# Three modulation vectors moved from the sets of steps 8 and 16 into those of steps 16, 32, 40 and 48

## The chip, the cores and the metric

The kernel runs on one core of one Trainium2 chip. The metric is the time of one execution on the device in microseconds (us); the median of several runs counts. The core has a matmul engine (TensorE, PE in the profile, PEld for its loads of weights), VectorE (DVE), ScalarE (ACT), GpSimd (POOL) and SyncE (SP), which issues nearly all DMAs here. The engines run side by side, each with its own queue in order, and wait for each other by semaphores.

## The reference

```python
def _A_ref(u, ...):                       # S4D: a long convolution along the 2048 tokens
    dt = exp(log_dt); A = -exp(log_A_real) + 1j * A_imag; C = (C_real + 1j * C_imag) * dt[:, None]
    P = exp((A * dt[:, None])[:, :, None] * pos)
    K = 2.0 * einsum("dn,dnl->dl", C, P).real            # 448 channels, 256 states, 2048 taps
    y = irfft(rfft(u_t, 4096) * rfft(K, 4096))[:, :, :2048]
    return y + u * D_skip
def _B_ref(x, w1, b1, w2, b2):            # mixer MLP along the tokens, 2048 -> 1792 -> 2048
    return (gelu(layernorm(x)^T w1 + b1) w2 + b2)^T

mod = (silu(c) @ w_mod).reshape(1, 6, 1, 448)
sa, ca, ga, sb, cb, gb = mod[:, 0], ..., mod[:, 5]
x = A_u                                                  # (1, 2048, 448)
x = x + ga * _A_ref(layernorm(x) * (1 + ca) + sa, ...)
x = x + gb * _B_ref(layernorm(x) * (1 + cb) + sb, ...)
```

The six vectors of 448 elements that `c` and `w_mod` (448 x 2688) give are the subject here: `mod[0]` to `mod[5]` are sa, ca, ga, sb, cb, gb. The first three are needed in the convolution, the last three (sb, cb, gb) in the MLP at the end.

## The kernel before

The first half of the kernel makes the taps K of the convolution for 28 groups of 16 channels, in 56 steps (`s` from 0 to 55, two for each group). Every eight steps (`BATCH`) form a set. At the start of a set stands a window: for each of its eight steps TensorE makes exponents (`st_exponents`, L687, through `halves`, L667), ScalarE takes their exponential (`st_exp`, L696, two of 128x512 for each step, tile `mag`), GpSimd makes `st_mag2` (L712, L717). The windows of steps 0, 8, 16, 24 and 32 are `window(s)`, those of 40 and 48 `late_window(s)`; `e` counts the eight passes. After it each step turns phases (`st_phase`, L667 again) into sines (`st_step`: ScalarE L729 to L735) and these into the tiles `E` (VectorE, L739 to L743) and `G` (GpSimd, L737, L738). `E` and `G` have three rooms each in the pool `gp_`. `st_kgen` (L764) multiplies them into PSUM two steps later (one step later from step 33 on), and `st_s1` (L802, L808) begins the Fourier transform of the taps.

Between these runs everything else, put by hand into the order of TensorE, ScalarE, VectorE and GpSimd:

- `chain(q)`, small VectorE work on the parameters of the next groups (`more(n)` takes its next n pieces; L415 to L489, split on GpSimd at L404 and L406, written to DRAM at L410). In the window its pieces stand between the passes.
- `u_rows` (L591 on TensorE, L595 on VectorE, written at L597 as `yu_d<-yt`, three tiles `yt`) in the steps from 8 to 16: the input's transform, which reads `mod[1]*mod[2]` and the tile `xt` of the input; then `u_cols` (L627, L631) from step 17, which reads `mod[0]*mod[2]` and what `u_load` (L617, tile `yi`) fetches.
- `pc_load` (L828, L841), `pc_s2` (L872), `pc_mul` (L880), `pc_inv` (L895) and `pc_out` (L905, L902) from step 33: the product of the two spectra and its inverse. `piece(...)` does one of these; in the late windows it stands in passes 3 and 5.
- `warm(n)` (L679) and `idle(n)` (L685): n matmuls on constants whose results nobody reads.

`act` and `dve` are lists of work that is put off to the next `flush`, which for the windows comes once in each pass. The PSUM pool `pms` (tag `ms`) has three rooms that the modulations, `u_rows`, `u_cols`, `st_s1` and the pieces share.

A modulation has two halves, `modulation(k, 0)` and `modulation(k, 1)`. The first multiplies a broadcast copy of silu(c) (`scb`) with the weights of vector k (four matmuls of 112 rows into four quarters of a PSUM tile `pm`, L537), and a copy takes it to the tile `parts` (L539). The second adds the four quarters by a matmul with `sums` (L533), and a copy takes it, with 1 added for k of 1 and 4, to `mod[k]` (L534). The weights are 784 KB for each k, loaded by `wm_load` (L341), for k of 0 to 2 into a tile that is reused for spectra later (`wm0`), for k of 3 to 5 into rows of `xt` that `u_rows` has read:

```python
if s == 8 and e in (3, 4):
    modulation(0, e - 3)
if s == 8 and e == 5:
    G.tensor_tensor(mod[0], mod[0], mod[2], ALU.mult)
for k, e0 in ((4, 1), (5, 3), (3, 6)) if s == 16 else ():
    if e in (e0, e0 + 1):
        modulation(k, e - e0)
```

Vectors 1 and 2 are made in steps 4 to 7. SyncE's order is written out by hand up to step 8; from there to the second half a planner orders its DMAs by when its own model of the kernel has them ready.

After the 56 steps come the rest of the spectral products, the layer norm with `mod[3]` and `mod[4]` (L1455, L1456) and the MLP (L1400 to L1402, L1563 to L1565), which take the second half of the time.

Of the kernel before, what the change touches and what calls it, by code (L numbers as in the profile page):

```python
# [11 lines left out]
F32 = mybir.dt.float32  # L12
F32R = mybir.dt.float32r
BF16 = mybir.dt.bfloat16
AF = mybir.ActivationFunctionType
# [7 lines left out]
P = 128  # L23
# [209 lines left out]
def tile_adaln_s4d_mixer(ctx, tc, i, out):  # L233
# [19 lines left out]
    with ExitStack() as es:  # L253
# [85 lines left out]
        def wm_load(k, tile):  # L339
            wms[k] = tile  # L340
            nc.sync.dma_start(wms[k], i["w_mod"][:, k * D : (k + 1) * D].rearrange("(q p) d -> p q d", p=PP))  # L341
# [11 lines left out]
        def wm_slot(k):  # L353
            w = wm0.rearrange("p k d -> p (k d)")[0:PP]
            return w[:, 4 * D * (k % 4) : 4 * D * (k % 4 + 1)].rearrange("p (q d) -> p q d", q=4)
# [3 lines left out]
        late = {  # L359
            4: lambda: wm_load(2, wm_slot(2)),  # L360
            7: lambda: [
                wm_load(0, wm_slot(0)),
                nc.sync.dma_start(svt, i["SV"]),
                s2_load(0),
                s2_load(1),
# [2 lines left out]
                nc.sync.dma_start(wu, i["WU"]),  # L368
                nc.sync.dma_start(wc, i["WC"].rearrange("p (c m) -> p c m", c=2)),
            ],  # L370
            12: lambda: wm_load(4, xt[0:PP, 0:4, 0:D]),
            13: lambda: wm_load(5, xt[0:PP, 4:8, 0:D]),
            14: lambda: wm_load(3, xt[0:PP, 8:12, 0:D]),
        }


        dt = qp.tile([P, 4], F32, name="dt")
# [140 lines left out]


        sc = qp.tile([PP, 4], F32, name="sc")  # L520
        scb = qp.tile([PP, 4, 32], F32, name="scb")
        sums = qp.tile([P, P], F32, name="sums")
        G.memset(sums, 0.0)
        for q in range(4):
            G.memset(sums[32 * q : 32 * q + 1], 1.0)
# [3 lines left out]
        def modulation(k, half):  # L529

            pm = pms.tile([P, D], F32, tag="ms", name="pm")
            if half:
                T.matmul(pm, sums, pmods.pop(k), start=True, stop=True)  # L533
                act.append(lambda: S.activation(mod[k], pm, AF.Copy, bias=1.0 if k in (1, 4) else 0.0))  # L534
                return
            for q in range(4):
                T.matmul(pm[32 * q : 32 * q + 32], scb[:, q], wms[k][:, q], start=True, stop=True)  # L537
            pmods[k] = qp.tile([P, D], F32, tag="parts", name="parts")
            act.append(lambda: S.copy(pmods[k], pm))  # L539


        mv = xp.tile([P, 16, 2], F32, name="mv")
# [131 lines left out]
        def warm(n):  # L674

            g = made_k[0] // 2
            free = (kgs[g - 1] if g - 1 in kgs else kg_tile(g))[:, 4:8]
            for _ in range(n):
                T.matmul(free, ones[:, 0:P], ones[:, 0:256], start=made_k[0] % 2 == 0, stop=made_k[0] % 2 == 0, skip_group_check=True)  # L679
# [392 lines left out]
        def late_window(s):  # L1072

            flush(hold)
            for e in range(BATCH):
                st_exp(s + e)
                if e + 1 < BATCH:
                    st_exponents(s + e + 1)
                else:
                    st_phase(s)  # L1080
                mellow()
                flush(dve)
                flush(act)
                if e == 1:
                    st_kgen(s - 1, dve)
                elif e in (3, 5):
                    piece(False, True)
                st_mag2(s + e)
            st_s1(dve)
            flush(dve)  # L1090

        def window(s):
            if s:
                aside.append(True)
            angle()
            logs(s == 8)
            if s == 8:
                more(10)
                u_scale()
                u_table(0)  # L1100
                u_table(1)

            if s == 0:
                st_exponents(s)
            for e in range(BATCH):
                st_exp(s + e)

                if e + 1 < BATCH:
                    st_exponents(s + e + 1)
                else:  # L1110
                    st_phase(s)
                mellow()
                flush(dve)
                flush(act)
                if s == 8 and e == 0:
                    tt(mod[1], mod[1], mod[2], ALU.mult)
                if s < 32:
                    more(WPACE[s // 8][e])
                if s == 0 and e >= 4:
                    u_stats(e - 4)  # L1120
                if s == 8 and e in (3, 4):
                    modulation(0, e - 3)
                if s == 8 and e == 5:

                    G.tensor_tensor(mod[0], mod[0], mod[2], ALU.mult)
                if s and e < (2 if s <= 32 else 1):
                    st_kgen(s - (2 if s <= 32 else 1) + e)
                elif e == 5 and s < 24:
                    if s == 8:
                        yks[0] = y0.tile([P, 32, DC], F32, tag="yk", name="yk0")  # L1130
                    st_s1(act)

                for k, e0 in ((4, 1), (5, 3), (3, 6)) if s == 16 else ():
                    if e in (e0, e0 + 1):
                        modulation(k, e - e0)

                if s == 8 and e == 0:
                    warm(7)
                if s == 8 and e == 1:
                    u_means()  # L1140
                if s in (8, 16):
                    some(u_rows, rows, ((0, 2, 2, 2, 2, 0, 2, 2) if s == 8 else (2, 2, 2, 2, 2, 0, 1, 1))[e])
                elif s == 24 and e in (0, 2, 4, 6, 7):
                    some(u_cols, cols, 1)

                if s == 0 and e > 1:
                    st_mag2(e - 2)
                elif s and (e < 2 or s >= 32):
                    st_mag2(s + e)
                if s == 0 and e == 3:  # L1150
                    for r in range(4):
                        dsk_copy(r)
            aside.clear()
            if s == 8:
                flush(dve)
            if s >= 24 and st_s1(dve):
                flush(dve)
            if s == 0:

                S.activation(one, one, AF.Sin)  # L1160
# [5 lines left out]
        for s in range(NHALF):  # L1166
# [33 lines left out]
            if True:  # L1200
                if s < 32 and s % BATCH > 1:
                    st_kgen(s - 2)
                if s % BATCH == 1 or s < 24 and s % BATCH == 0:
                    warm(10)
                if (s + 1) % BATCH:
                    st_phase(s + 1)
                elif s + 1 < NHALF:
                    st_exponents(s + 1)
                if s == 7:
                    warm(10)  # L1210

                due.extend(soon)
                soon.clear()
                if s > 32 and s % BATCH:
                    st_kgen(s - 1, soon)
                if s in (40, 48):
                    piece(True)
                    flush(dve)
                st_step(s, between)
                if s in (40, 48):  # L1220
                    piece(False, True)
# [3 lines left out]

            if s in (1, 2):
                x_load(4 + 4 * s, 4, G)
            if s in (23, 31):
                idle(10)
            held = s > 32 and s % BATCH == BATCH - 2  # L1230
# [366 lines left out]
```

## Time and profile before

| what | value |
|---|---|
| runs | 663.93, 664.15, 666.26 us; median 664.15 |
| profiled execution | 663.85 us, span 662.1 us |
| mean clock granted to TensorE | 0.984 |
| busy, of the span | PE 612.3 us (92%), PEld 442.9, DVE 443.0 (67%), ACT 439.9 (66%), POOL 269.5 (41%) |
| weights of modulations | 6 loads of 784 KB, issued by SyncE between 32.9 and 106.1 us |
| matmuls of modulations | L537 x48 and L533 x12, from 43.4 to 131.2 us |

The span is the time from the first to the last instruction. Times in rows are in us from the start of the span. A row of the timeline has start, length, engine, line, operation, tile written and tiles read, shape and count, and in brackets how long the engine stood idle before it and what ended that. A row of the chain has start, length and the piece of work: it is the sequence of work that ended last, followed back from the end, so only what stands on it makes the kernel longer. A row of busy times has a stretch, its length, for each engine the busy us and the number of instructions, the share of the clock that TensorE got, and the mean share of the DMA engines with their GB/s (a share over 1 comes from counting a transfer where it starts). The letter q behind an engine means its queue.

### The profile page before, as it was taken

The numbers are of one execution on the slowest core, as the hardware profiler recorded it, in microseconds if no ns is written. First come the engines' busy times: TensorE is split into PE (matmuls) and PEld (weight loads), VectorE is DVE, ScalarE is ACT, GpSimd is POOL, SyncE is SP. The second block draws the span as 40 slices with busy tenths as digits, with TensorE's granted clock in tenths as the row PEclk, the third lists the DMA queues.
The fourth block names the chain that finished last, engine by engine and source line by source line (L and its number), as shares of the span: only waits on it lengthen the run. The fifth ranks groups of instructions, "written<-read, shape, count | busy, mean of one in ns | idle before, by whom it ended". The sixth has DMA issues, their size and how long they took to land.

```text
span 662.1 us, 19161 instructions
## 1 busy us (share of the span) xinstructions
PE 612.3 (92%) x7639; PEld 442.9 (67%) x7639; DVE 443.0 (67%) x853; ACT 439.9 (66%) x828; POOL 269.5 (41%) x351
## 2 busy tenths in 40 slices
PE   1878998999999999999888999999999999999997
PEld 0444555445455565656544577788999999999996
DVE  8989889689894887868655688777422553333331
ACT  5978888899989999999587678885222522222220
POOL 7785597588599788787563000000000000000000
PEclk9998999989999999999999899999999999999999
DMA  6595747598775557576787999946755275555530
GB/s 145 156 219 166 253 143 257 182 248 268 218 247 178 103 166 218 169 215 182 234 274 227 257 247 234 233 112 196 201 160 153 57 209 164 162 160 166 161 106 28
DMA packets 97858, 123.67 MB, mean 187 GB/s; under 512 B 13717, under 2 KB 79801, under 8 KB 97769
## 3 DMA queue, kind: packets, MB, share of 16 engines
q1 hardware_dynamic: 97032, 120.02, 64.2%
q0 software_dynamic: 736, 2.43, 1.5%
q8 instruction: 60, 0.98, 0.7%
q14 instruction: 30, 0.24, 0.1%
HBM read 88.33 MB, written 33.59 MB: 184 GB/s over the span
## 4 chain that ended last, share of the span: by engine, by line
PE 63%; DMA 11%; DVE 9%; ACT 7%; POOL 4%; issue 4%; SPq 3%; ACTq 0%; DVEq 0%; POOLq 0%
PE o L1563 7%; PE o L1565 7%; PE o L1564 7%; PE acc L1400 6%; PE acc L1401 6%; PE acc L1402 6%; PE xe L667 6%; PE kg L764 6%; DMA w<-in_B_w_dram 3%; PE xg L667 3%; DMA xt<-in_A_u_dram 3%; DMA v_d<-vt 3%; PE pu L591 2%; PE vv L895 2%; PE kx L872 2%
## 5 line engine op out<-in xcount | busy, mean ns | idle before, releaser
L218 ACT CAST whi<-w 128x896 fp32r<-128x896 f32 x64 | 59.7, 939 | 138.5 <-PE o L1564 82.7
L227 DVE TENSOR_TENSOR wlo<-w,whi 128x896 fp32r<-128x896 f32 x64 | 68.1, 1086 | 41.4 <-ACT whi L218 35.1
L737 POOL TENSOR_TENSOR G<-mag,gs 128x512 f32<-128x512 f32 x56 | 71.9, 1283 | 36.4 <-ACT gs L733 36.4
L1400 PE MATMUL acc<-h3h,whi 128*128 128x448 f32 x224 | 83.0, 371 | 1.7 <-ACT h3h L1467 0.9
L1401 PE MATMUL acc<-h3l,whi 128*128 128x448 f32 x224 | 81.4, 363 | 0.5 <-DVE h3l L1474 0.3
L1563 PE MATMUL o<-uh,whi 128*128 128x448 f32 x224 | 81.3, 363 | 0.0
L1565 PE MATMUL o<-uh,wlo 128*128 128x448 f32 x224 | 81.2, 362 | 0.0
L1402 PE MATMUL acc<-h3h,wlo 128*128 128x448 f32 x224 | 81.0, 361 | 0.0
L1564 PE MATMUL o<-ul,whi 128*128 128x448 f32 x224 | 80.6, 360 | 0.0
L764 PEld LDWEIGHTS kg<-E,G 128*32 128x32 f32 x3584 | 56.2, 114 | 33.1 <-issue 18.4
L738 POOL TENSOR_TENSOR G<-mag,gs 128x512 f32<-128x512 f32 x56 | 71.9, 1285 | 0.0
L764 PE MATMUL kg<-E,G 128*32 128x64 f32 x3584 | 65.9, 227 | 6.4 <-issue 4.2
L667 PE MATMUL xg<-tab,lph 64*128 64x512 f32 x112 | 62.0, 553 | 6.6 <-DVE E L743 4.3
L1568 DVE TENSOR_TENSOR y<-o,x 128x448 f32<-128x448 f32 x16 | 10.0, 624 | 79.0 <-PE o L1565 79.0
L667 PE MATMUL xe<-tab,lph 64*128 64x512 f32 x112 | 61.9, 553 | 0.3 <-issue 0.2
L717 POOL TENSOR_TENSOR m<-mag,w 128x512 f32<-128x512 f32 x53 | 55.8, 1053 | 4.2
L1400 PEld LDWEIGHTS acc<-h3h,whi 128*128 128x128 f32 x224 | 42.0, 188 | 14.8 <-issue 2.1
L729 ACT ACTIVATE ab<-xe 128x512 f32<-128x512 f32 x56 | 33.9, 604 | 16.3 <-PE xg L667 9.1
L1401 PEld LDWEIGHTS acc<-h3l,whi 128*128 128x128 f32 x224 | 42.0, 187 | 3.8 <-DVE h3l L1474 0.9
L1565 PEld LDWEIGHTS o<-uh,wlo 128*128 128x128 f32 x224 | 42.1, 188 | 3.4
L1402 PEld LDWEIGHTS acc<-h3h,wlo 128*128 128x128 f32 x224 | 42.0, 187 | 3.1
L1564 PEld LDWEIGHTS o<-ul,whi 128*128 128x128 f32 x224 | 41.9, 187 | 3.0
(257 smaller groups left out, 1399.1 us busy)
## 6 DMA issues: line engine op xcount, KB each, us to landing
w<-in_B_w_dram SPq DMA_DIRECT2D x64, 224.0 KB
w<-in_B_w_dram SPq DMA_DIRECT2D x32, 448.0 KB
yi<-yu_d SPq DMA_DIRECT2D x32, 224.0 KB
us_d<-uo SPq DMA_DIRECT2D x16, 448.0 KB
u<-us_d SPq DMA_DIRECT2D x64, 112.0 KB
v_d<-vt SPq DMA_DIRECT2D x32, 224.0 KB
vt<-v_d SPq DMA_DIRECT2D x14, 448.0 KB
yu_d<-yt SPq DMA_DIRECT2D x13, 448.0 KB
```

Source lines behind the costliest of these rows:

```text
L218: self.nc.scalar.copy(hi, w)
L227: eng.tensor_tensor(lo, w, hi.bitcast(F32), ALU.subtract)
L667: T.matmul(out[k], lhs[r], rhs[r], start=start, stop=stop)
L737: G.tensor_tensor(Gt[:, 1], mg_, v32(sg), ALU.mult)
L738: G.tensor_tensor(Gt[:, 0], mg_, v32(cg_), ALU.mult)
L764: T.matmul(kg[32 * q : 32 * q + 32, m], Gt[:, c, d], E[:, c, d], start=h == 0 and c == 0 and m == 0, stop=h == 1 and c == 1, skip_group_ch ...
L1400: nc.tensor.matmul(acc[f], hi[:, fs], h3h[:, r], start=r == 0, stop=False)
L1401: nc.tensor.matmul(acc[f], hi[:, fs], h3l[:, r], start=False, stop=False)
L1402: nc.tensor.matmul(acc[f], lo[:, fs], h3h[:, r], start=False, stop=r == 15)
L1563: nc.tensor.matmul(o, hi[:, ks], uh[kh][:, k], start=kh == 0 and k == 0, stop=False)
L1564: nc.tensor.matmul(o, hi[:, ks], ul[kh][:, k], start=False, stop=False)
L1565: nc.tensor.matmul(o, lo[:, ks], uh[kh][:, k], start=False, stop=kh == 1 and k == 6)
```

## The change

- Vector 0: its weights are loaded at step 12 into the rows of `xt` that vector 4 had, not at step 7; its halves stand in passes 1 and 2 of the window of step 16, and its product with `mod[2]` on GpSimd in pass 4 there.
- Vectors 4, 3 and 5: their halves stand in passes 4 and 6 of the windows of steps 32, 40 and 48. `wm_room` takes one of the three rooms of `E` for the weights, at the end of steps 31, 38 and 46. Both copies go to VectorE, and `parts` lies in the room `ab` of `st_step`.
- `scb` and `sums` move to a pool that lives longer.
- The ten warming matmuls at the end of step 7 (`warm(10)`) go.

```diff
         late = {
             4: lambda: wm_load(2, wm_slot(2)),
             7: lambda: [
-                wm_load(0, wm_slot(0)),
                 nc.sync.dma_start(svt, i["SV"]),
...
-            12: lambda: wm_load(4, xt[0:PP, 0:4, 0:D]),
-            13: lambda: wm_load(5, xt[0:PP, 4:8, 0:D]),
-            14: lambda: wm_load(3, xt[0:PP, 8:12, 0:D]),
+            12: lambda: wm_load(0, xt[0:PP, 0:4, 0:D]),
         }
+        def wm_room(k):
+            E = gp_.tile([P, 2, GD, NJ], F32, tag="E", name="wE")
+            wm_load(k, E.rearrange("p a g j -> p (a g j)")[0:PP, 0 : 4 * D].rearrange("p (q d) -> p q d", q=4))
+        last_mods = {32: 4, 40: 3, 48: 5}
...
-        scb = qp.tile([PP, 4, 32], F32, name="scb")
-        sums = qp.tile([P, P], F32, name="sums")
+        scb = cg.tile([PP, 4, 32], F32, name="scb")
+        sums = cg.tile([P, P], F32, name="sums")
...
                 T.matmul(pm, sums, pmods.pop(k), start=True, stop=True)
-                act.append(lambda: S.activation(mod[k], pm, AF.Copy, bias=1.0 if k in (1, 4) else 0.0))
+                one_more = 1.0 if k in (1, 4) else 0.0
+                if k > 2:
+                    dve.append(lambda: ts(mod[k], pm, one_more, None, ALU.add))
+                else:
+                    act.append(lambda: S.activation(mod[k], pm, AF.Copy, bias=one_more))
                 return
...
-            pmods[k] = qp.tile([P, D], F32, tag="parts", name="parts")
-            act.append(lambda: S.copy(pmods[k], pm))
+            if k > 2:
+                parts = wp.tile([P, 512], F32, tag="ab", name="parts", bufs=1)[:, 0:D]
+            else:
+                parts = qp.tile([P, D], F32, tag="parts", name="parts")
+            pmods[k] = parts
+            (dve if k > 2 else act).append(lambda: (V.tensor_copy if k > 2 else S.copy)(parts, pm))
...
+                if e in (4, 6):
+                    modulation(last_mods[s], (e - 4) // 2)
                 st_mag2(s + e)
...
-                if s == 8 and e in (3, 4):
-                    modulation(0, e - 3)
-                if s == 8 and e == 5:
+                if s == 16 and e == 4:
                     G.tensor_tensor(mod[0], mod[0], mod[2], ALU.mult)
...
-                for k, e0 in ((4, 1), (5, 3), (3, 6)) if s == 16 else ():
-                    if e in (e0, e0 + 1):
-                        modulation(k, e - e0)
+                if s == 16 and e in (1, 2):
+                    modulation(0, e - 1)
+                if s == 32 and e in (4, 6):
+                    modulation(last_mods[s], (e - 4) // 2)
...
-                if s == 7:
-                    warm(10)
...
+            if s in (31, 38, 46):
+                wm_room(last_mods[s + BATCH - s % BATCH])
```

## The prediction, made before the changed kernel was run

> **What bounds the kernel now.** I read the page first, then the chain of work that ended last in order of time, then the timeline around every place that the diff touches, and last the busy times by stretch and SyncE's own queue.
>
> ```profile
> span 662.1 us, 19161 instructions
> PE 63%; DMA 11%; DVE 9%; ACT 7%; POOL 4%; issue 4%; SPq 3%; ACTq 0%; DVEq 0%; POOLq 0%
> ```
>
> TensorE is 63% of the chain, but which engine ends the work differs from set to set, and the change moves work between sets. So each place has to be read by itself. First set 8 (windows of eight exponentials, about 58 to 80 us), where the first vector is made now:
>
> ```profile
> 58.41 1.21 PE kg L679 x10
> 59.64 0.37 ACT L778 COPY ks<-kg 128x256 f32<-128x256 f32 x1 [1.38 <-PE kg L679]
> 70.66 0.89 PE pm L537 x8
> 72.73 0.95 PE pm L533 x2
> 72.53 1.28 DVE L595 SCALAR_TENSOR_TENSOR yE<-pu,means,mod 128x448 f32<-128x448 f32 x2 [1.12 <-PE pu L591]
> 74.66 1.28 DVE L595 SCALAR_TENSOR_TENSOR yE<-pu,means,mod 128x448 f32<-128x448 f32 x2 [0.86 <-PE pu L591]
> 75.09 1.14 POOL L1125 TENSOR_TENSOR mod<-mod,mod 128x448 f32<-128x448 f32 x1
> 75.86 0.66 DVE L457 TENSOR_TENSOR s<-xa,ya 128x256 f32<-128x256 f32 x1
> ```
>
> The rows with only a start, a length and a name are the chain: both halves of the modulation (L537, L533) lie on it, and right behind each VectorE waits for TensorE. The ten warming matmuls (L679) lie on it too, and ScalarE waits for them. Now the busy times by stretch:
>
> ```profile
> core 0: us, PE busy (x) PEld busy (x) DVE busy (x) ACT busy (x) POOL busy (x), PEclk, DMA share, GB/s
> 47.40:50.80 3.40, 2.28 (x17) 1.06 (x17) 3.33 (x8) 1.14 (x3) 2.27 (x3) 0.89 0.89 162
> 50.80:54.20 3.40, 3.40 (x74) 2.18 (x72) 3.33 (x8) 2.79 (x6) 2.00 (x2) 0.61 0.18 60
> 57.60:61.00 3.40, 2.84 (x14) 1.56 (x14) 3.33 (x8) 2.01 (x6) 2.85 (x4) 1.00 0.58 176
> 61.00:64.40 3.40, 2.40 (x72) 1.73 (x72) 3.16 (x10) 3.36 (x7) 0.00 (x0) 1.00 1.03 276
> 64.40:67.80 3.40, 2.47 (x70) 1.78 (x72) 3.22 (x9) 3.40 (x8) 2.33 (x4) 1.00 0.75 242
> 134.80:138.20 3.40, 2.14 (x13) 1.00 (x11) 2.53 (x5) 3.40 (x8) 3.32 (x4) 1.00 1.08 225
> 138.20:141.60 3.40, 3.40 (x68) 1.74 (x70) 2.77 (x5) 3.37 (x8) 3.32 (x5) 0.58 1.10 242
> 202.00:214.00 12.00, 11.13 (x225) 6.69 (x224) 3.77 (x6) 11.48 (x22) 11.47 (x18) 0.99 0.54 155
> 243.00:252.00 9.00, 8.97 (x142) 4.95 (x142) 4.43 (x10) 8.88 (x18) 8.14 (x14) 1.00 0.56 148
> 281.00:293.00 12.00, 11.81 (x209) 6.80 (x206) 5.82 (x13) 11.94 (x23) 10.81 (x18) 1.00 0.72 211
> ```
>
> From 57.6 to 67.8 VectorE is busy 9.71 of 10.2 us (3.33 + 3.16 + 3.22): it is the bound at the start of set 8. At 243 and 281, in the sets that get new work, TensorE has almost nothing free (8.97 of 9.00) and VectorE more than half.
>
> **The change part by part.** One modulation is eight 112-row and two 128-row matmuls and two copies of 128x448:
>
> ```profile
> L539 ACT COPY parts<-pm x6: 532/544/564, 46.4 to 130.1; 128x448 f32<-128x448 f32 x6
> L534 ACT ACTIVATE mod<-pm x6: 543/547/553, 53.0 to 135.4; 128x448 f32<-128x448 f32 x6
> ```
>
> So it is worth 0.89 + 0.95 = 1.84 us of TensorE and 0.54 + 0.55 = 1.09 us of ScalarE, besides 784 KB of weights. Moving it to VectorE has no exact row; the nearest, L595, takes 1.28 for two, 0.64 each, and I take 0.6.
>
> *Set 8.* It loses one modulation, the multiplication on GpSimd (1.14), and the ten warming matmuls. The warming matmuls: ScalarE could take ks 1.38 us earlier, and the exponentials of set 8 with it. But VectorE goes on without a gap until 68.5, so nothing comes out at that point: I take 0 for them, with ends +0.5 (cold clock, below) and -0.6 (TensorE's lead used up later). The modulation: 1.84 us leave TensorE ahead of VectorE's two waits, which sum to 1.98; without it the pairs of rows (0.5 us each) follow VectorE directly, and the L457 at 75.86, that follows the second pair, moves up by some 1.7. L457 ran 0.66 beside GpSimd's product; the same form took 0.43 elsewhere (L445, quoted below), so 0.2 to 0.3 more comes back. I take -2.0 for set 8, ends -1.2 (VectorE finds other waits) and -2.5.
>
> *Steps 9 to 15.* Two of three 784 KB loads into xt go. One of them stands in the chain's way:
>
> ```profile
> 96.04 0.37 SPq L341 DMA_DIRECT2D xt<-in_w_mod_dram  x1
> 96.50 7.72 DMA yu_d<-yt
> 102.88 1.01 PE L591 MATMUL pu<-xt,wur 64*128 64x448 f32 x2
> 104.32 1.27 DVE L595 SCALAR_TENSOR_TENSOR yt<-pu,means,mod 128x448 f32<-128x448 f32 x2 [1.50 <-DMA yu_d<-yt]
> ```
>
> The write of yt is issued right behind the load, and VectorE waits for its room until 104.32. At the 242 to 276 GB/s of the stretches above, 784 KB are about 3 us, so the write would land near 101. What is late next is TensorE: the first pu of that pair cannot be read before some 103.4 (102.88 + 0.5). Gain 0.9, ends -0.3 and -1.2. The other load, at 106, and the first vector's old one at 59 end no wait on the chain: 0.
>
> *Set 16.* Three modulations become one (that of mod[0], with its product on GpSimd); 2 x 1.84 us of TensorE and 2 x 1.09 us of ScalarE go.
>
> ```profile
> 128.69 0.43 DVE L445 TENSOR_TENSOR xa<-xa,u 128x256 f32<-128x256 f32 x1
> 130.12 0.56 ACT L539 COPY parts<-pm 128x448 f32<-128x448 f32 x1
> 131.18 0.29 DVE L457 TENSOR_TENSOR s<-xa,ya 128x128 f32<-128x128 f32 x1 [2.06 <-ACT ya L451]
> 138.54 0.20 PEld L627 LDWEIGHTS pu<-yi,s 64*64 64x64 f32 x6 [0.39 <-DMA yi<-yu_d]
> ```
>
> VectorE's own run to L445 does not shorten (the product may lengthen it by 0.4). ScalarE ends 1.5 earlier (three copies of 0.54 gone ahead of the set's end), and of VectorE's 2.06 us wait 1.5 go. But at 138.54 TensorE waits for yi, whose loads are issued behind the set's splits in SyncE's queue and are bound by DMA (share 1.08 and 1.10 in those stretches). They do not move by themselves, unless SyncE's order brings them forward now that xt is read out earlier. So the gain is 0.2 to 1.5, and with an earlier order up to 2: I take -0.8.
>
> *Set 32.* It gets a modulation between its exponentials, with both copies on VectorE, which is 3.77 of 12 us busy. ScalarE paces this set (six exponentials in 3.04 us, 0.51 each; TensorE waits 0.31 for each):
>
> ```profile
> 205.71 3.04 ACT mag L696 x6
> 201.52 0.50 SPq L657 DMA_DIRECT2D lph<-pars  x1
> 207.01 2.15 SPq L828 DMA_DIRECT2D u<-us_d  x4
> 212.58 0.18 PEld L667 LDWEIGHTS xe<-tab,lph 64*128 64x128 f32 x1 [0.31 <-ACT mag L696]
> 214.12 0.60 ACT L729 ACTIVATE ab<-xe 128x512 f32<-128x512 f32 x1
> ```
>
> A half of 0.9 us between two exponents (0.5 us for both, when both rooms are free) fits in ScalarE's 1.0 us a step, and the second half runs just ahead of the phase (four passes, 1.3 us in set 40, where they end at 251.74 in the rows below), which started at 212.58 and would start at 213.4: ab at 214.12 becomes 214.6, +0.5 (ends 0 and +0.9). The weights: SyncE is free from 202.0 to 207.0, because the loads of u wait there; a load issued then lands by 207 and is needed at 210.6. It waits for the room of the E of step 29, which is read by step 31.
>
> *Sets 40 and 48.* Both have two inverse pieces in TensorE's order as well:
>
> ```profile
> 248.62 0.49 PE xg L667
> 249.11 0.92 PE vv L895 x16
> 251.30 0.44 PE xg L667 x2
> 251.62 0.60 ACT L729 ACTIVATE ab<-xe 128x512 f32<-128x512 f32 x1
> ```
>
> Putting the halves in by hand: exponents of e=5 end at 248.2, the first half at 249.1, exponents of e=6 at 249.5, the piece at 250.5, exponents of e=7 at 250.9, the second half at 251.8, the phase at 253.2 instead of 251.74. Some 0.4 us are absorbed in waits for ScalarE, 1.45 stay; ends 0.9 and 1.84. In set 48 the same order gives 1.45 again. Behind both sets TensorE is on the chain without a break, so it is not given back. VectorE's 1.2 us fall in idle time. PSUM: the first half takes the room that z has left, the piece the other two. E: three rooms remain three, the next E takes one whose products were made a step before, so it costs nothing; the loads have 8 us to land, at a DMA share of 0.56 to 0.72. Their issue is 0.4 us of SyncE each.
>
> Sum: -2.0 - 0.9 - 0.8 + 0.5 + 1.45 + 1.45 = -0.3. The profiled execution took 663.85 us (span 662.1), so 663.55; it lies 0.3 below the median shown, 664.15. I say 663.6.
>
> **The clock.** At 134.8 TensorE was busy 2.14 of 3.40 us and got 0.58 of its clock in the next stretch; at 47.4 it was 2.28 and then 0.61. Without the warming matmuls the stretch from 57.6 has 2.84 - 1.2 = 1.6, less than both, so a cold stretch at 61 or 64 is likely. It costs 2.4 us of TensorE (the 2.40 of one stretch once more) against idle time of 1.0 and the lead of 1.4, so 0 to 0.5 on the chain; -2.0 has some 0.4 of that in it. If the clock stays full there, set 8 gives -2.4 and the whole 663.2; within the forecast I give that 4 in 10. The Trainium skill, "TensorE: Matmul & The Clock Gate", section "Why this matters for your kernels", names only idle gaps above about 3 us between bursts as what brings the half clock; here no gap that long would arise, so by it the clock would stay full and set 8 would give the larger gain. The two rows above speak against so mild a rule, since the stretches ahead of a drop were busy for over 2 of 3.4 us.
>
> **The rivals.**
> *Faster, 0.25.* The gain in the early sets passes whole: set 8 -2.5, the write -1.2, set 16 -2.0 because the yi loads come earlier, -5.7 in all; the cold stretch at 138 (0.58 of the clock over 3.4 us, so at most 1.4 of TensorE's time) may go as well, -1.2. Late, the sets absorb more: +2.3 to +3.1 (0.5 + 0.9 + 0.9 at the least). Together -2.6 to -4.6, so 659.2 to 661.2. For it: every wait named ended last where it stands. Against it: VectorE's run at 57 to 68 and the DMA at 138.
> *Slower, 0.13.* SyncE's order puts the load of set 32 behind the loads of u. Then it is issued at 209.2 (207.01 + 2.15) and shares the DMA with them; it lands at 214 or later instead of by 210.6, and TensorE, ScalarE behind it, stand 3.5 to 5 us: 667 to 668.6. It decides as soon as the load is issued later than about 206. Against it: SyncE idles 5 us there and the load's room is free before 202.
> *Early gains small, 0.12.* Sets 8 and 16 are VectorE's and give 1.2 together, the write 0.3: +1.9, 665.7.
> *The forecast, 0.50:* 661.2 to 666.
>
> **How the numbers follow.** About 0.5% (3.3 us) is what a measurement of this kernel can tell from no change. Against 664.15, faster is below 660.8: four fifths of the first rival, 0.20. Slower is above 667.5: two thirds of the second rival, and part of the third with the late prices at their ends (0.9 and 1.84 twice: +3.1 instead of +1.9, and more where the clock falls), 0.13. The rest, 0.67, is within. The range, 659.6 to 667.8, takes in both outer rivals but for their far ends; the likeliest case alone is 661.2 to 666.
>
> **What would show it.** In the profile after: no L533 at 72, VectorE's L595 without the waits of 1.12 and 0.86, L457 near 74; the write of yt landing in under 5 us and the L595 wait of 1.50 gone; L457 in set 16 closer to L445, and L627 still behind a DMA; in sets 40 and 48 the span from the first exponential to ab longer by 1.45 us each, in set 32 by 0.5; the load of set 32 issued ahead of the first u. Wrong would be: TensorE's wait on a w_mod load in any late set, a set 40 that is not longer, or set 8 less than 1 us shorter.

## The result: 18 us slower, and the profile after

| | before | after |
|---|---|---|
| runs, us | 663.93, 664.15, 664.90, 666.26 | 682.12, 682.94, 684.14 |
| ratio after to before | | 1.0275, 95% interval 1.0243 to 1.0306 (+18.3 us) |
| profiled execution, span | 663.85, 662.1 | 682.12, 680.3 |

One more run of the changed kernel took 3078.56 us at full clock, and one of a later version (v1_one_late) 674.24; both count as slow and are left out of the ratios and medians.

Lines of the changed kernel stand lower in its file: the halves of a modulation are L545 (before L537) and L537 (before L533), the exponential L708, the first sine pass L741. The tile `wE` is the room of `E` that holds the weights of a late vector. First the page of the kernel after, its span and the chain's shares by engine:

```profile
span 680.3 us, 19118 instructions
...
PE 53%; DMA 12%; ACT 11%; DVE 8%; POOL 8%; issue 5%; SPq 1%; ACTq 0%; POOLq 0%; DVEq 0%
```

TensorE's share of the chain was 63% before and is 53%, while ScalarE's went from 7 to 11% and GpSimd's from 4 to 8%: more of the chain now runs outside TensorE. The chain in order of time, around the sets of steps 40 and 48 (start, length, piece of work):

```profile
238.94 7.15 DMA v_d<-vt
...
246.16 8.64 DMA wE<-in_w_mod_dram
...
254.94 1.72 PE pm L545 x8
...
257.38 1.70 PE vv L907 x16
...
262.19 0.60 ACT ab L741
...
291.68 1.21 DVE yk L820 x2
...
292.95 8.36 DMA wE<-in_w_mod_dram
...
301.44 1.72 PE pm L545 x8
...
309.30 0.60 ACT ab L741
```

Read it downwards. A write of v_d is issued at 238.94 and lands 7.15 us later. Only then does SyncE issue the load of the weights (L341 at 246.16), which takes 8.64 us to land. Only then does TensorE start the modulation, and its first half takes 1.72 us where the prediction had 0.89. In set 48 the load takes 8.36 us and TensorE starts behind it in the same way, but what the load itself waited for last is VectorE's work on yk, not v_d (more below). TensorE's own timeline (in brackets the idle time ahead and what ended it), at the first halves:

```profile
208.65 1.39 PE L545 MATMUL pm<-wE,scb 112*32 112x448 f32 x8 [1.72 <-DMA wE<-in_w_mod_dram]
...
254.94 1.72 PE L545 MATMUL pm<-wE,scb 112*32 112x448 f32 x8 [4.33 <-DMA wE<-in_w_mod_dram]
...
301.44 1.72 PE L545 MATMUL pm<-wE,scb 112*32 112x448 f32 x8 [4.62 <-DMA wE<-in_w_mod_dram]
```

The prediction named "TensorE's wait on a w_mod load in any late set" as what would make it wrong. Here it is in all three: 1.72 + 4.33 + 4.62 = 10.7 us. Behind the wait comes the clock; busy times by stretch, the third entry from the right (PEclk) is the share of the clock that TensorE was granted:

```profile
244.00:250.00 6.00, 5.80 (x88) 3.04 (x88) 1.90 (x4) 4.35 (x9) 4.35 (x9) 0.72 0.68 180
250.00:254.00 4.00, 0.60 (x6) 0.18 (x2) 0.69 (x2) 1.27 (x3) 3.26 (x5) 0.93 1.07 220
254.00:258.00 4.00, 3.06 (x18) 1.06 (x22) 0.62 (x1) 0.54 (x2) 0.00 (x0) 0.50 0.48 145
```

From 250 to 254 TensorE is busy 0.60 of 4 us, and in the next stretch it gets half its clock: vv (the matmuls of an inverse piece) takes 1.70 us on the chain, at 257.38, where the kernel before had 0.92 for it.

How much each late set grew: from its first exponential to its first sine pass. ScalarE's timeline of the kernel before (its other ends, 205.71, 214.12 and 251.62, stand in the prediction) and of the kernel after, whose last two ends, 262.19 and 309.30, stand in the chain above:

```profile
243.36 0.60 ACT L696 ACTIVATE mag<-xe 128x512 f32<-128x512 f32 x1
...
281.32 0.60 ACT L696 ACTIVATE mag<-xe 128x512 f32<-128x512 f32 x1
...
289.58 0.60 ACT L729 ACTIVATE ab<-xe 128x512 f32<-128x512 f32 x1
```

```profile
202.03 0.60 ACT L708 ACTIVATE mag<-xe 128x512 f32<-128x512 f32 x1
...
213.97 0.60 ACT L741 ACTIVATE ab<-xe 128x512 f32<-128x512 f32 x1 [1.06 <-issue]
...
243.21 0.60 ACT L708 ACTIVATE mag<-xe 128x512 f32<-128x512 f32 x1
...
291.67 0.60 ACT L708 ACTIVATE mag<-xe 128x512 f32<-128x512 f32 x1
```

| set | before | after | growth |
|---|---|---|---|
| 32 | 205.71 to 214.12: 8.41 | 202.03 to 213.97: 11.94 | +3.5 |
| 40 | 243.36 to 251.62: 8.26 | 243.21 to 262.19: 18.98 | +10.7 |
| 48 | 281.32 to 289.58: 8.26 | 291.67 to 309.30: 17.63 | +9.4 |

Together +23.6. At the start of set 32 the changed kernel was 3.7 us ahead (202.03 against 205.71), and between the sets and after them it gains some 1.7, which leaves the 18.2 of the spans. So the early part went as forecast in its sum, and the late part cost 23.6 instead of 3.4.

Why the loads are late is seen in SyncE's queue of the kernel after (DMA issues, start and length):

```profile
201.90 0.32 SPq L840 DMA_DIRECT2D u<-us_d  x1
202.34 0.71 SPq L341 DMA_DIRECT2D wE<-in_w_mod_dram  x1
...
238.94 0.38 SPq L921 DMA_DIRECT2D v_d<-vt  x1
240.09 2.30 SPq L840 DMA_DIRECT2D u<-us_d  x4
243.80 0.36 SPq L853 DMA_DIRECT2D si<-in_SI_dram  x1
244.20 0.43 SPq L665 DMA_DIRECT2D lph<-pars  x1
245.53 0.50 SPq L669 DMA_DIRECT2D lph<-pars  x1
246.16 0.34 SPq L341 DMA_DIRECT2D wE<-in_w_mod_dram  x1
...
284.91 0.38 SPq L921 DMA_DIRECT2D v_d<-vt  x1
```

In set 32 the load goes out behind the first u, and the other loads of u and si go out with it; TensorE's wait for it ends at 208.65, 6.3 us after the issue. In set 40 the program asks for the load at the end of step 38, but the planner put it behind the write of v_d, four loads of u, one of si and two of lph. In the trace SyncE's DMAs raise eight semaphores in turn, and before one of them is raised again SyncE waits until the DMA that raised it last, eight places ahead, has landed. The load into the room of E stands exactly eight places behind v_d, so it inherits the 7.15 us of that write. In set 48 one more DMA (yk) stands between, and the load is ninth behind v_d (284.91): there the load of lph just ahead of it is the one that waits for v_d, until 292.00, and the load then waits for VectorE's yk until 292.89.

### The profile page after: what moved, and what is told of

It reads as the page before. It is cut to its first block, busy times and chain, and to the rows that moved or that the text cites. A ratio compares the mean times of both kernels' runs of the same rounds, so it can differ in the third digit from the quotient of the medians.

```text
span 680.3 us, 19118 instructions
## 1 busy us (share of the span) xinstructions
PE 616.5 (91%) x7629; PEld 441.9 (65%) x7629; DVE 448.9 (66%) x859; ACT 437.7 (64%) x822; POOL 270.3 (40%) x351
## 4 chain that ended last, share of the span: by engine, by line
PE 53%; DMA 12%; ACT 11%; DVE 8%; POOL 8%; issue 5%; SPq 1%; ACTq 0%; POOLq 0%; DVEq 0%
PE o L1576 7%; PE o L1575 7%; PE o L1577 7%; PE acc L1412 6%; PE acc L1413 6%; PE acc L1414 6%; PE kg L776 3%; PE xe L679 3%; POOL G L749 3%; DMA w<-in_B_w_dram 3%; DMA v_d<-vt 3%; POOL G L750 3%; DMA wE<-in_w_mod_dram 2%; PE xg L679 2%; ACT gs L745 2%
## 5 line engine op out<-in xcount | busy, mean ns | idle before, releaser
L776 PEld LDWEIGHTS kg<-E,G 128*32 128x32 f32 x3584 | 54.3, 112 | 30.3 <-issue 18.6
L776 PE MATMUL kg<-E,G 128*32 128x64 f32 x3584 | 63.4, 224 | 4.1 <-issue 2.6
L708 ACT ACTIVATE mag<-xe 128x512 f32<-128x512 f32 x56 | 34.4, 614 | 23.9 <-issue 14.1
L741 ACT ACTIVATE ab<-xe 128x512 f32<-128x512 f32 x56 | 33.8, 603 | 17.7 <-PE xg L679 8.5
L1575 PEld LDWEIGHTS o<-uh,whi 128*128 128x128 f32 x224 | 42.1, 188 | 3.4
```

What stands on the lines that cost most here:

```text
L776: T.matmul(kg[32 * q : 32 * q + 32, m], Gt[:, c, d], E[:, c, d], start=h == 0 and c == 0 and m == 0, stop=h == 1 and c == 1, skip_group_ch ...
L1575: nc.tensor.matmul(o, hi[:, ks], uh[kh][:, k], start=kh == 0 and k == 0, stop=False)
```

## The experiments

In the table each ratio is against runs of the kernel before on the same chip, whose medians were 664.53 (first four), 665.45 (next four) and 664.63 us (last four).

| kernel | median, us | ratio, 95% interval |
|---|---|---|
| e2_no_late | 665.54 | 1.0023 (0.9997 to 1.0049) |
| e3_no_load | 666.49 | 1.0021 (0.9989 to 1.0053) |
| e4_load_only | 671.14 | 1.0123 (1.0081 to 1.0164) |
| e1_act_queue | 674.13 | 1.0155 (1.0109 to 1.0201) |
| e2b_no_late | 662.75 | 0.9943 (0.9913 to 0.9974) |
| e6_act_early | 668.60 | 1.0031 (1.0001 to 1.0061) |
| e7_sync_early | 669.44 | 1.0058 (1.0030 to 1.0085) |
| v2_all_16 | 665.87 | 1.0008 (0.9983 to 1.0033) |
| e5_before_no_warm | 665.78 | 1.0020 (0.9990 to 1.0049) |
| e8_before_no_load13 | 663.42 | 0.9978 (0.9949 to 1.0006) |
| v1_one_late | 665.77 | 1.0005 (0.9975 to 1.0034) |
| v2_two_late | 667.54 | 1.0034 (1.0006 to 1.0061) |

The traces gave this growth of the late sets against the kernel before, taken as in the table above:

| kernel | set 32 | set 40 | set 48 |
|---|---|---|---|
| after | +3.5 | +10.7 | +9.4 |
| e3_no_load: work without loads | +0.6 | +1.5 | +1.5 |
| e4_load_only: loads without work | 0.0 | +1.2 | +2.3 |
| e1_act_queue | +5.9 | +1.6 | +1.5 |
| e6_act_early | +0.9 | +1.6 | +3.6 |
| e7_sync_early | +0.6 | +2.7 | +3.9 |
| e2_no_late: neither | +0.7 | 0.0 | 0.0 |
| e2b_no_late: neither | 0.0 | 0.0 | 0.0 |

**The early part alone.** Two kernels without the three late vectors:

```diff
-                if e in (4, 6):
-                    modulation(last_mods[s], (e - 4) // 2)
...
-            if s in (31, 38, 46):
-                wm_room(last_mods[s + BATCH - s % BATCH])
+            if s in (31, 38, 46):                                   # e2b only
+                V.memset(mod[last_mods[s + BATCH - s % BATCH]], 1.0)
```

> Vectors 3, 4 and 5 are not computed (their mod is set to 1.0 and their weights are not loaded); the early part of the change (vector 0 in set 16, sets 8 and 16 relieved, no warming matmuls of step 7) stays. All theories put the loss into the sets 32 to 48, where the traces diverge, so here the gain of the early sets stands alone: phases run 3.7 us ahead of the kernel before at the start of set 32, so 660.8 (664.5 - 3.7), between 660 and 662. If part of that lead is given back in sets 24 to 55 for another reason (a wait for a DMA that does not move), 662 to 664.5.

> As e2_no_late (vectors 3, 4 and 5 not computed, no late loads), but their mod is set to 1.0 by VectorE at the end of steps 31, 38 and 46; in e2_no_late the same three fills at the kernel's beginning made the start 3.9 us later (sines of step 1 at 36.59 instead of 32.65), which hid the gain. With that out of the way the early gain should show: 660.8 (664.5 - 3.7), between 660 and 662.5. If the gain of the early sets is not real or is given back: 664 or more.

The first missed: it fills the three vectors at the kernel's beginning, and that cost as much as was to be seen. With the fills moved to where VectorE has room, the early part is worth 0.57% (0.26 to 0.87), 3.8 us: the 3.7 of the prediction's first three terms.

**The work alone.** The late matmuls read a constant tile instead of weights:

```diff
-T.matmul(pm[32 * q : 32 * q + 32], scb[:, q], wms[k][:, q], ...)
+T.matmul(pm[32 * q : 32 * q + 32], scb[:, q], (wms[k][:, q] if k < 3 else tab[0:PP, q % 3, 0:D].bitcast(F32)), ...)
...
-            if s in (31, 38, 46):
-                wm_room(last_mods[s + BATCH - s % BATCH])
```

> The matmuls and copies of vectors 3 to 5 stay in the sets of steps 32, 40 and 48, but read a constant tile: no late weight loads and no room of E taken. Theory A: what is left is the TensorE work, 0.5 + 1.45 + 1.45 us on top of 660.8: 664 (662.5 to 665.5). Theory B: the TensorE work itself is the price: 676 to 682. Theory C: as A, since the loads are gone.

ScalarE's timeline of e3, first exponential and first sine pass of the three sets:

```profile
204.71 0.60 ACT L708 ACTIVATE mag<-xe 128x512 f32<-128x512 f32 x1
...
213.73 0.60 ACT L741 ACTIVATE ab<-xe 128x512 f32<-128x512 f32 x1 [0.63 <-ACT mag L708]
...
243.97 0.60 ACT L708 ACTIVATE mag<-xe 128x512 f32<-128x512 f32 x1
...
253.71 0.60 ACT L741 ACTIVATE ab<-xe 128x512 f32<-128x512 f32 x1 [0.96 <-ACT mag L708]
...
283.30 0.60 ACT L708 ACTIVATE mag<-xe 128x512 f32<-128x512 f32 x1
...
293.03 0.60 ACT L741 ACTIVATE ab<-xe 128x512 f32<-128x512 f32 x1 [0.96 <-ACT mag L708]
```

They take 9.02, 9.74 and 9.73 us: +0.6, +1.5 and +1.5. The prediction had +0.5, +1.45 and +1.45. The median, 666.49, lies above the 664 expected; by ratios the work costs 1.0021 - 0.9943 = 0.8% (0.3 to 1.2, adding the two uncertainties in squares), 5.2 us, of which the three sets account for 3.6. That the added TensorE work makes most of the loss is ruled out.

**The loads alone.** The mirror image: rooms and loads stay, nobody multiplies (with e2_no_late's fills, so e2_no_late is what it is compared with).

```diff
-                if e in (4, 6):
-                    modulation(last_mods[s], (e - 4) // 2)
```

> The loads into the rooms of E stay on SyncE, but vectors 3 to 5 are not multiplied (their mod is set to 1.0), so nobody reads what is loaded. Theory A: no wait of TensorE, only the sharing of the DMA and, where the room of E comes free late, a short wait of VectorE: 661 to 663.5. Theory B: as A. Theory C: the loads of u and si land late, and pieces behind them: 668 to 676.

All theories that held the loads to be free beside TensorE's wait fell here: 1.0% above e2_no_late (0.5 to 1.5), 5.6 us by medians. The traces put 3.5 of it into sets 40 and 48, where neither e2 kernel has any. So the loads have a price of their own. Where it comes from is not shown: the time lies in the range of theory C, but in set 48 no engine waits for a DMA, and TensorE's granted clock is 0.59 from 290 to 294.

**Another queue, and one step earlier.**

```diff
-            wm_load(k, ...)                                         # e1 and e6
+            wms[k] = E.rearrange(...)[0:PP, 0 : 4 * D].rearrange(...)
+            S.dma_start(wms[k], i["w_mod"][:, k * D : (k + 1) * D].rearrange(...))
...
-            if s in (31, 38, 46):                                   # e6 and e7
+            if s in (30, 37, 45):
```

> The three late weight loads are issued from ScalarE's queue, at the place in ScalarE's order where the steps 31, 38 and 46 end, not by SyncE; all else as in the changed kernel (682.1 us in its profile). Theory A (the load comes late because it is placed late in SyncE's order; TensorE stands on it for 10.7 us in three places, ScalarE behind it, and the TensorE clock falls): the loads go out some 8 to 10 us earlier, the waits of L545 on w_mod are below 1 us in sum, and the time is 664 to 667. Theory B (the added matmuls and copies cost it in sets whose TensorE is full, and the load is late only because everything is late): stays at 678 or above. Theory C (784 KB more on the DMA queues delay the loads of u and si, whichever engine issues them): 670 to 678, with the waits moved from w_mod to u and si.

> Late loads from ScalarE's queue as in e1_act_queue, and each one step earlier (ends of steps 30, 37 and 45). In e1 the sets of 40 and 48 cost only some 1.4 us each, but set 32 cost 7.7: its load went out at 200.1, beside the loads of u and si, and took 9.3 us. Theory A (collision of that load with the loads of u and si, which begin at 201.9): some 3 to 4 us earlier it has landed before most of them are out; set 32 then costs 1.6 (as with no load at all in e3), and the time is 664.5 to 667. Rival (784 KB more in set 32 delay the loads of u and si and the instructions' own fetches whenever they are issued): 669 to 673 as in e1, 674 in its runs.

> The changed kernel with one thing altered: the rooms for the weights are taken at the end of steps 30, 37 and 45 instead of 31, 38 and 46, and the loads stay on SyncE. In SyncE's order the load then stands right behind the write v_d in sets 40 and 48 (six and seven places earlier) and ahead of the first u in set 32. Theory A (the place in SyncE's order behind eight DMAs, of which the load must wait for the landing of v_d, 7.2 us, makes it late): issued near 240 and 286 instead of 246.2 and 293, landing 8 us later, just in time; TensorE's waits on w_mod fall from 10.7 us to under 3, and the time is 665 to 669. Rival (the waits come from the loads' own time and the added TensorE work, not from their place): 676 or more.

e1 takes away the waits of sets 40 and 48, which grow by 1.6 and 1.5 us, no more than with no load at all. But its set 32 is the worst of all kernels, and its time, 674.13, misses theory A and lies in the range of theory C. The chain there, and TensorE's timeline:

```profile
200.06 9.32 DMA wE<-in_w_mod_dram
```

```profile
206.37 0.76 PE L777 MATMUL kg<-E,G 128*32 128x64 f32 x37 [2.00 <-issue]
...
209.51 1.72 PE L546 MATMUL pm<-wE,scb 112*32 112x448 f32 x8 [0.28 <-DMA wE<-in_w_mod_dram]
```

Issued at 200.06 the load needs 9.32 us, beside the loads of u and si, and the halves then run on a slow clock. But TensorE waits only 0.28 us for it. Before that it stands idle for 2.00 us in the middle of the kg matmuls, with no wait that the profile names (`issue`); what caused that is not shown. e6, with the load out at 195.9, has +0.9 in that set, where the first theory of e6 said 1.6; its set 48 then grew by 3.6, which stays open, and its time was somewhat above what was expected.

e7 is the cleanest: against the changed kernel only three step numbers differ, and SyncE still issues. SyncE's queue and TensorE's timeline of e7 in set 40:

```profile
240.09 0.38 SPq L921 DMA_DIRECT2D v_d<-vt  x1
241.11 0.65 SPq L341 DMA_DIRECT2D wE<-in_w_mod_dram  x1
```

```profile
250.18 0.96 PE L545 MATMUL pm<-wE,scb 112*32 112x448 f32 x8 [1.11 <-DMA wE<-in_w_mod_dram]
```

The load now goes out 1 us behind v_d and not 7.2, because it stands next to it in the order and no longer eight places on. It still takes some 9 us to land, and TensorE waits 1.11 instead of 4.33. In sets 32 and 48 it does not wait for w_mod at all. The time falls from 1.0275 to 1.0058 of the kernel before: 2.2% (1.8 to 2.6), 14.4 us, hang on the loads' place in the queue; the median, 669.44, is just above the 669 that was expected at most. In set 32 that is no more than an issue one step earlier; in sets 40 and 48 it also frees the load from v_d.

**The early terms, one by one, on the kernel before.**

```diff
-                if s == 7:                                          # e5
-                    warm(10)
...
-            13: lambda: wm_load(5, xt[0:PP, 4:8, 0:D]),             # e8
...
-T.matmul(..., wms[k][:, q], ...)
+T.matmul(..., wms[4 if k == 5 else k][:, q], ...)
```

> The kernel before with one part of the change alone: the ten warming matmuls at the end of step 7 are gone. The prediction took 0 for them, with ends +0.5 (a cold stretch at 61 to 64) and -0.6 (TensorE's lead): 664.5 plus or minus 0.6 beside its kernel before. In the trace: ks about 1.4 us earlier, and the granted clock between 57 and 68 either full (then the prediction's case of a cold stretch is wrong) or near 0.6. Rival (the gain of the early sets is mostly theirs, because ScalarE starts set 8 earlier): -2, and the sines after set 8 about 2 us earlier.

> The kernel before without the weight load of step 13: vector 5 is computed from the weights of vector 4, so its values are not those of the reference; all instructions but that one DMA stay. The prediction gave the loss of this load -0.9 (ends -0.3 and -1.2), by the write of yt behind it that landed after 7.72 us. If that holds: the sines of step 14 come 0.9 to 1.6 us earlier than in the kernel before, VectorE's wait of 1.50 us for the write of yt is gone, and the time is 663.3 (beside 664.5). Rival: in v2_all_16, where such a load stands at the same place, the wait was gone too and step 14 had gained 1.4 us; then the load is not its cause, and nothing is gained here: 664.5.

Busy times of e5 in two stretches of the prediction, and TensorE's timeline there:

```profile
57.60:61.00 3.40, 2.09 (x5) 0.66 (x4) 3.33 (x9) 3.38 (x8) 3.10 (x4) 1.00 0.62 164
61.00:64.40 3.40, 2.74 (x66) 2.11 (x67) 3.16 (x11) 3.36 (x8) 0.48 (x1) 0.50 1.01 254
```

```profile
61.66 0.79 PE L667 MATMUL xg<-tab,lex 64*128 64x512 f32 x1 [0.95 <-DVE E L743]
```

Without the warming matmuls the granted clock falls to 0.50 from 61 to 64.4 (1.00 in the kernel before), and the first sine pass of step 8 comes 0.9 us later (79.88 against 78.98). The time, +0.2% (-0.1 to +0.5), can't tell 0 from 1 us. e8 gives -0.2% (-0.5 to +0.1), so it decides nothing by itself either; its trace has the wait for yt gone. But so has that of e5, which keeps the load. SyncE's queue of e5:

```profile
94.84 0.42 SPq L341 DMA_DIRECT2D xt<-in_w_mod_dram  x1
96.15 3.91 SPq L597 DMA_DIRECT2D yu_d<-yt  x2
```

The load goes out 1.3 us ahead of the write (96.15), not 0.5 us as in the profile of the kernel before (96.04 and 96.50), and nothing waits. So the row of 1.50 us was real, but the wait can go with the load still there. What decides it, the microsecond of the issue or something else, one trace of each kernel can't tell.

**Versions meant to beat both.**

```diff
+            14: lambda: [wm_load(4, xt[0:PP, 4:8, 0:D]), wm_load(5, xt[0:PP, 8:12, 0:D])],   # v2_all_16
+                for k, e0 in ((0, 1), (4, 3), (5, 5), (3, 6)) if s == 16 else ():
+                    if e in (e0, e0 + 1):
+                        modulation(k, e - e0)
+            if s == 15:
+                wm_room(3)                                          # load from ScalarE
...
+                for k, e0 in ((0, 1), (4, 3), (5, 6)) if s == 16 else ():    # v1_one_late
+            if s == 37:                                             # only vector 3 late, in set 40
...
+                for k, e0 in ((0, 1), (4, 3)) if s == 16 else ():   # v2_two_late
+            if s in (37, 45):                                       # vectors 3 and 5 late
```

> A version that may beat both: vectors 0, 4, 5 and 3 all in the window of step 16 (passes 1 and 2, 3 and 4, 5 and 6, 6 and 7), nothing late. Weights of 0, 4 and 5 go to rows of xt at steps 12 and 14, those of 3 into a room of E at the end of step 15 from ScalarE's queue; no modulation in set 8. In the trace of the changed kernel TensorE is busy only 1.31 of 6 us from 128 to 134, waiting for yi, so the three modulations should mostly fall into time that is lost anyway. Theory: early gain of 3.7 us less 0 to 2 us: 661 to 663. If set 16 has no room for them: each modulation costs up to 1.84 us of TensorE, 664 to 667.

> A version that may beat both: as the changed kernel in the early sets, but vectors 4 and 5 stay in set 16 (passes 3, 4 and 6, 7, behind vector 0 in 1 and 2), and only vector 3 is late, in set 40, with its room of E taken at the end of step 37 and its load on SyncE. By the traces set 16 took the same time with one modulation (after) and with three (before), and a late set costs 1.3 (work) to 2.5 us (with its load, e7): 664.5 - 3.7 + 2 = 662.8, range 661.5 to 665. If three in set 16 cost what they cost in v2 (some 4 us for four): 665.

> As v1_one_late, but vector 5 late too, in set 48, with its room at the end of step 45; only 0 and 4 in set 16. Sets 40 and 48 cost 2.5 and 3.7 us in e7: 664.5 - 3.7 + 6.2 = 667; if the loads cost nothing beside set 32's, 1.3 each: 663.4. Range 663 to 667.5.

None beats the kernel before, and the first two lie above what was expected of them. With four modulations in set 16 they do not fall into idle time; the chain of v2_all_16 there:

```profile
128.75 0.56 ACT parts L553
...
129.35 1.02 PE pm L539 x2
130.37 0.89 PE pm L547 x8
```

ScalarE's copies and TensorE's halves follow each other on the chain, and the set ends 4.8 us later than with three. v1_one_late had 3.5 us in hand at the start of set 32 in its profile and lost 2.4 in set 40; in its runs nothing is left, 1.0005 (0.9975 to 1.0034). With two late vectors it is 1.0034. No version that makes all six vectors kept an early gain that the runs can tell from nothing.

## Why the prediction was wrong, point by point

It said 663.6 us, range 659.6 to 667.8; the time is 683.

*The step that failed* is "the loads have 8 us to land, at a DMA share of 0.56 to 0.72". That assumed that the load goes out where the step ends that asks for it. In set 40 it went out 7.2 us after the v_d that it should have followed, in set 48 8.0 us after, and then took 8.64 and 8.36. Nor are 8 us enough: in e7 the load went out at 241.11, right behind v_d, TensorE's first half began at 250.18, and 1.11 us of the time between were a wait for the load. The prediction had looked at SyncE's queue in set 32 only and carried the result over to sets 40 and 48.

In set 32 the load went out about when it was forecast (202.34, forecast from 202.0), so the condition of the rival "SyncE's order", a load issued later than about 206, did not come true. What failed there is "lands by 207 and is needed at 210.6". TensorE waited for it until 208.65, and needed it 1.72 us before that, because the early gain had moved the set 3.7 us forward and the load not at all. The first half then took 1.39 us. That the set grew by 3.5, the low end of that rival's 3.5 to 5, is luck. The rival's mechanism, a load that stands behind other DMAs in SyncE's order, came true in sets 40 and 48, where the prediction had not placed it.

The rows that would have told were in the trace before, in SyncE's queue:

```profile
238.66 0.38 SPq L909 DMA_DIRECT2D v_d<-vt  x1
...
245.33 1.79 SPq L828 DMA_DIRECT2D u<-us_d  x4
```

The first of these u stands eight places behind v_d, and by the semaphore events of that trace v_d landed at 245.15, 6.5 us after its issue. The Trainium skill says of such writes ("Perfetto Trace Analysis", section "DMA Instruction — HWDGE (DVE, Sync)") that the completion "can cause a surprisingly long delay especially when the write target is HBM", and that a DMA which looks fast in the profile may still be waiting for the DMA engines. The trace agrees: v_d and the load of weights are issued in 0.38 and 0.34 us and land after 7.15 and 8.64. But not every such write is slow: a v_d issued at 259.85 landed after 2.1 us, by the semaphore events.

*The second size that was missed* is the clock in the late sets. The prediction weighed it for set 8 and not there. In set 40 the growth of 10.7 is 1.5 of work and 4.33 of waiting; most of the remaining 4.9 is matmuls that take up to twice their time (1.72 for 0.89, 1.70 for 0.92). About half of it, 2.4, stands behind the wait: from the first half to the first sine pass it is 7.25 us (254.94 to 262.19), and 4.87 in e3 (248.84 to 253.71), whose first half is this row of TensorE's timeline:

```profile
248.84 0.96 PE L545 MATMUL pm<-tab,scb 112*32 112x448 f32 x8
```

The other 2.5 stand ahead of the wait, from 244 to 250, where the clock was already 0.72; so the wait is not what lowered it there, and what did is open.

*Sets 32, 40 and 48, the work:* +0.5, +1.45, +1.45 forecast, +0.6, +1.5, +1.5 in e3. Right. VectorE's copies took 0.625 each (0.6 forecast).

*Set 8:* VectorE's timeline after, in set 8 and, in the last row, in set 16:

```profile
71.75 2.46 DVE L607 SCALAR_TENSOR_TENSOR yE<-pu,means,mod 128x448 f32<-128x448 f32 x4
74.16 0.42 DVE L461 TENSOR_TENSOR s<-xa,ya 128x256 f32<-128x256 f32 x1
...
127.76 0.29 DVE L461 TENSOR_TENSOR s<-xa,ya 128x128 f32<-128x128 f32 x1 [1.91 <-ACT ya L455]
```

The waits of 1.12 and 0.86 are gone, and the row that was L457 at 75.86 is L461 at 74.16: 1.7 earlier, and 0.42 long, both as written. The warming matmuls were taken at 0; e5 shows them to be worth 0.5 to 0.9 us in its profile, so the modulation gave somewhat more than forecast and the clock took it back. The cold stretch itself came where it was expected (0.50 from 61 to 67.8 in e5). The rule that the Trainium skill has for it ("TensorE: Matmul & The Clock Gate", section "Why this matters for your kernels", idle gaps above about 3 us) would have left the clock full: in e5 the longest idle time of TensorE between 52 and 62 is 0.95 us, and the clock fell by half. The measurement decides.

*Steps 9 to 15:* 0.9 forecast and found, but for a reason that e5 shows to be loose. The 3 us that a load of 784 KB was given there are too few: the load at 96.04 landed 7.1 us later, by the semaphore events of the same trace.

*Set 16:* forecast 0.8, found 0.3 to 0.4. VectorE still waits 1.91 us for ScalarE at 127.76 (2.06 before), and TensorE has nothing to do; its timeline after:

```profile
131.94 0.76 PE L679 MATMUL xe<-tab,lph 64*128 64x512 f32 x1 [4.55 <-ACT gs L746]
```

v1_one_late, with three modulations in that set as before, lost nothing against one. TensorE's time there was free, and the two vectors that the change took away had cost nothing that the profiles show. That the three early terms sum to what e2b gave is therefore in part luck.

*The account in the runs' terms:* -3.8 for the early part (e2b), +5.2 for the late work (e3 less e2b), +2.5 for loads that are about in time (e7 less e3, uncertain by 2.8), +14.4 for their place in the queue (after less e7): +18.3. Each term is a difference of two kernels in a row, so the sum closes by construction; each is uncertain by 2 to 3 us.

*What the profiles can't tell:* one profile of unchanged code differs from the next by 1 to 3 us. e5 lost 0.7 in set 32 and e2b 1.0 in the steps 33 to 39, where neither has a reason to; e4 took some 3 us longer than e2_no_late in set 24, ahead of the first step in which the two differ, 1.75 of it in one idle time of TensorE that no wait explains, like the 2.00 in e1. Terms below that are read from the runs or not at all.

## What to carry to other kernels

A load that is moved has to be priced from the moment at which its queue can issue it: list what stands ahead of it in that queue, in every place that it is moved to, and how long the DMA that it must wait for (here the one eight places ahead) takes to land. Work that is moved can be priced well from the rows of its instructions (here within 0.15 us a set), but TensorE paid twice here for waiting on data, with the wait and with the slow clock behind it. And ask whether the place that is relieved had any need: set 16's two modulations had cost nothing where they were.

## What was not expected of the hardware

- TensorE's clock fell to 0.50 with no idle gap longer than 0.95 us, while it was busy 2.09 of 3.40 us (e5).
- 784 KB took 8.4 to 9.3 us to land, from SyncE's queue (8.36, 8.64) and from ScalarE's (9.32) alike: some 90 GB/s beside the other traffic. The quickest late load of the changed kernel took some 6 us (set 32), where the prediction had taken 3 us for such a load from a stretch's total of 242 to 276 GB/s.
- The landing of v_d that cost so much is that of a small part of it: a DMA's semaphore rises in sixteen steps, and for the v_d at 238.94 fourteen had come within 2.9 us and the last two only after 7.1 (at 284.91: 2.8 and 7.1).
- Fills that nobody waits for shift a start: with three fills of 128x448 on VectorE at the kernel's beginning the sines of step 2 came 3.9 us later (36.65 against 32.71, e2_no_late) and 4.3 us later (37.05, e4_load_only). The expectation of e2b calls that step 1. Why they come later is open.
